# Exp in a windowed attention: the order in which its input is read and its output is written

## The chip, the cores and the metric

The kernel runs on one core of one Trainium2 chip. The metric is the device time of one launch in microseconds (us). "Before" was timed in six runs. One further execution was recorded by the hardware profiler; every duration, wait and timeline row below comes from that one.

## The reference, cut to what matters

Eight batches of eight heads, 576 positions, 64 values per head. Each position attends to the positions at most 32 away. The attention output, 4608 tokens of 512 values, goes through a two-layer network.

```python
scores = (1/sqrt(64)) * q @ k.T
scores = where(abs(pos_q - pos_k) <= 32, scores, -1e9)
attn   = exp(scores - max(scores));  attn = attn / (sum(attn) + 1e-9)
x      = attn @ v                    # -> 4608 tokens x 512
h      = x @ w_in                    # 512 -> 2048
g      = s * relu(h)**2 + b
out    = g @ w_out                   # 2048 -> 512
```

The kernel leaves out the subtraction of the maximum (the scores are small) and divides by the sum after the product with v.

## The kernel before, in words

**Attention.** A unit (`unit(b, m)`, L534) makes up to 128 tokens of batch `b`; a batch has five units, and eight batches make 40. A unit has an even key tile and, except in the last unit of a batch, an odd one, of 64 keys each. For a key tile, TensorE (PE) multiplies the keys of a pair of heads, laid out block-diagonally in `KBD` so that 2 x 64 keys fill the 128 partitions, with the queries of its window `QT`: four matmuls (L543), one for each pair of heads, into one of the two banks of the PSUM tile `SC`. A window has 128 queries, or 96 in the first and last tile of a batch. ScalarE (ACT) then takes the exponential of the whole bank and writes bf16 into the SBUF tile `EXE` (even) or `EXO` (odd): this is L560, the line that changes, 72 instructions in all. In batches 2 to 7 VectorE (DVE) multiplies the result by the band mask in place (L564); in batches 0 and 1 the mask was added beforehand by a matmul (L549). PE multiplies the weights with v into `AVN` (L582; 8 or 12 matmuls to a unit); DVE takes the reciprocal of the sums (L592) and scales (L595); the result is transposed into `XT`, the input of the network: by PE and an ACT copy (L604, L607) for batches 0 and 1, by a DMA (L612) later.

**Why the queries are in two runs.** The queries are loaded two to a partition, and the two are transposed apart. `QT` therefore holds the even queries of a batch first and the odd ones after them (index `i`), and the matmul leaves a window's scores in PSUM in that order, for each pair of heads: `w/2` scores of the even queries, then `w/2` of the odd ones. The tiles `EXE` and `EXO`, the mask and everything after them have the queries in their natural order. L560 is the instruction that passes from the one order to the other.

**Network.** `s1` (L687): PE multiplies 512 tokens with 128 columns of `w_in` (4 matmuls, L698) into one of two PSUM banks `W`, ACT takes the relu into `R1` (L705), DVE squares it into `GT` (L707). `W` has two banks, so a group of L698 can start only when the relu of the group before last is done. `s2` (L711): PE multiplies `GT` with `w_out` in groups of 4 matmuls (L717) into `O`, DVE scales and adds a constant (L730), a DMA stores. The first three token blocks (128, 128 and 256 tokens) are worked while the weights still arrive; the other eight blocks have 512 tokens.

**Order.** Each of the five instruction streams has a fixed order, which is written at build time by a planner (`_Graph`) from costs given with each operation: for L560 the cost is `190 + 0.833 * 4 * w` (ns), where four pairs of `w` scores make one partition's elements. At run time every engine works through its stream in order and waits on semaphores. On the ACT stream exps stand between the relus and, in batches 0 and 1, between copies and casts (`qt` L479, `kbd` L490, `vbd` L445, `win` L419, `xt` L607).

Of the kernel before, what the change touches and what calls it, by code (L numbers as in the profile page):

```python
# [7 lines left out]
AF = mybir.ActivationFunctionType  # L8
# [34 lines left out]
class _Graph:  # L43
# [12 lines left out]
    def add(self, stream, fns, cost, reads=(), writes=(), key=0.0, accum=False, dma=None, waits=(),  # L56
            lat=None, slack=0.0):
        if not isinstance(fns, list):
            fns = [fns]
        t = _Task(len(self.tasks), stream, fns, cost, self.LAT[stream] if lat is None else lat, key,  # L60
                  dma, slack)
        t.deps.update(waits)
        for r in reads:
            assert r in self.writer, r
            t.deps.add(self.writer[r])
        for w in writes:
            if w in self.writer:
                t.deps.add(self.writer[w])
            if not accum:
                t.deps.update(self.readers.get(w, ()))  # L70
        t.deps.discard(t)
        for r in reads:
            self.readers.setdefault(r, []).append(t)
        for w in writes:
            self.writer[w] = t
            if not accum:
                self.readers[w] = []
        self.tasks.append(t)
        return t
# [157 lines left out]
def bass_sliding_window_symmetric__then__act_starrelu_kernel(  # L237
# [22 lines left out]
    with ExitStack() as es:  # L260
# [65 lines left out]
        def unit_rows(m):  # L326
            lo = max(0, 128 * m - WIN)
            return lo, min(S, 128 * m + 128 - WIN)

        def due(b, m):  # L330
            tok = b * S + unit_rows(m)[0]
            blk = next(x for x in range(NM) if TBLK[x][0] + TBLK[x][1] > tok)
            f = (tok - TBLK[blk][0]) / TBLK[blk][1]
            before = PH[blk] - PH[blk - 1] if blk > 0 else 4.0
            return PH[blk] - 14.0 - (1.0 - f) * before
# [62 lines left out]
        def pieces(lo, hi, step):  # L398
            return range(lo // step, (hi - 1) // step + 1)
# [131 lines left out]
        def xt_res(t0, t1):  # L531
            return [("XT", x % (XR // 32)) for x in range(t0 // 32, t1 // 32)]

        def unit(b, m):  # L534
            slot, key = b % 2, due(b, m)
            n = ucount["n"]
            ucount["n"] += 1
            ei, pi = n % NEX, (n - 1) % NEX
            tiles = [j for j in (2 * m, 2 * m + 1) if j < NTILE]
            for j in tiles:  # L540
                lo, hi = max(0, 64 * j - WIN), min(S, 64 * j + 64 + WIN)
                c0, w, par = lo - (64 * j - WIN), hi - lo, j % 2
                fns = [lambda e, j=j, pr=pr, lo=lo, hi=hi, w=w, par=par: e.matmul(  # L543
                    SC[:, par, pr * 128:pr * 128 + w],
                    lhsT=KBD[:, pr, j, :], rhs=QT[slot][:, :, pr, lo // 2:hi // 2], start=b > 1,
                    stop=b > 1 or pr == NPAIR - 1) for pr in range(NPAIR)]
                src = SC[:, par, :].rearrange("p (a c) -> p a c", c=128)[:, :, 0:w]
                if b < 2:
                    fns.insert(0, lambda e, src=src, c0=c0, w=w: e.matmul(  # L549
                        src.rearrange("p a (i c) -> p a i c", i=2), lhsT=IDENT[:, :],  # L550
                        rhs=MASKB.rearrange("p a (i c) -> p a i c", i=2)[:, :, :, c0 // 2:(c0 + w) // 2],
                        start=True, stop=False))
                add("pe", fns, (8 if b < 2 else 4) * (w / 2.4 + 3.0),
                    reads=[("QT", slot, x, i) for x in pieces(lo, hi, 64) for i in (0, 1)]
                    + [("KBD", j, p0, i) for p0 in (0, 64) for i in (0, 1)]
                    + (["IDENT"] + [("MASKB", pr) for pr in range(NPAIR)] if b < 2 else []),
                    writes=[("SC", par)], key=key, slack=1500.0)
                src = src.rearrange("p a (i c) -> p a i c", i=2)
                dst = (EXE[ei][:, :, c0:c0 + w], EXO[ei][:, :, 64 + c0:64 + c0 + w])[par]
                add("act", lambda e, src=src, dst=dst: e.activation(  # L560
                    dst.rearrange("p a (c i) -> p a i c", i=2), src, AF.Exp, bias=0.0, scale=0.125),
                    190 + 0.833 * 4 * w, reads=[("SC", par)], writes=[("E", ei, par)], key=key)
                if b > 1:
                    add("dve", lambda e, dst=dst, c0=c0, w=w: e.tensor_tensor(  # L564
                        dst, dst, MASK[:, :, c0:c0 + w], ALU.mult),
                        130 + 0.53 * 4 * w, reads=[("E", ei, par), "MASK"], writes=[("E", ei, par)], key=key)
            r0, r1 = unit_rows(m)
            nr = r1 - r0
            lead = 0 if r0 == 128 * m - WIN else WIN
            av, avr = AVN, ["AVN"]  # L570
            if b == 0 and m % 2:
                av, avr = O.rearrange("p i (a c) -> p (i a) c", a=2), [("O", 0), ("O", 1)]
            fns = []
            for pr in range(NPAIR):
                parts = []
                if m > 0:
                    parts.append((EXO[pi], 128, 2 * m - 1))
                parts.append((EXE[ei], lead, 2 * m))
                if 2 * m + 1 < NTILE:
                    parts.append((EXO[ei], lead, 2 * m + 1))  # L580
                for x, (buf, col, j) in enumerate(parts):
                    fns.append(lambda e, pr=pr, buf=buf, col=col, j=j, x=x, last=len(parts) - 1: e.matmul(  # L582
                        av[0:nr, pr, 0:130], lhsT=buf[:, pr, col:col + nr],
                        rhs=VBD[slot][:, j, pr, 0:130], start=(x == 0), stop=(x == last)))
            vx = {int(j > 3) for j in tiles} | ({int(2 * m - 1 > 3)} if m > 0 else set())
            add("pe", fns, len(fns) * 57.0,
                reads=[("E", ei, j % 2) for j in tiles] + ([("E", pi, 1), ("EXZ", pi, 192)] if m > 0 else [])
                + [("EXZ", ei, 0), ("EXZ", ei, 192)] + [("V", slot, p0, x) for p0 in (0, 64) for x in vx]
                + [(r, slot, p0) for r in ("VBDZ", "VBDO") for p0 in (0, 64)], writes=avr, key=key)
            land["av", b, m] = g.tasks[-1]  # L590
            ri, xi = n % 2, n % NXN
            add("dve", lambda e: e.reciprocal(REC[ri][0:nr, :].rearrange("p (a b) -> p a b", b=2),  # L592
                                              av[0:nr, :, 128:130]),
                210, reads=avr, writes=[("REC", ri)], key=key)
            add("dve", lambda e: e.tensor_tensor(  # L595
                XN[xi][0:nr, :].rearrange("p (a b c) -> p a b c", a=4, b=2),
                av[0:nr, :, 0:128].rearrange("p a (b c) -> p a b c", b=2),
                REC[ri][0:nr, :].rearrange("p (a b one) -> p a b one", b=2, one=1).to_broadcast((nr, 4, 2, 64)),
                ALU.mult),
                680, reads=avr + [("REC", ri)], writes=[("XN", xi)], key=key)  # L600
            x0 = b * S + r0
            if b < 2:
                view = av.bitcast(BF16)[:, :, 384:512]
                add("pe", [lambda e, pr=pr: e.transpose(  # L604
                    view[:, pr, 0:nr], XN[xi][0:nr, pr * 128:(pr + 1) * 128], IDENT[0:nr, 0:nr])
                    for pr in range(NPAIR)], 300, reads=[("XN", xi), "IDENT"], writes=avr, key=key)
                add("act", lambda e: e.copy(XT[:, :, x0:x0 + nr], view[:, :, 0:nr]), 190 + 0.833 * 4 * nr,  # L607
                    reads=avr, writes=xt_res(x0, x0 + nr), key=key)
            else:
                cuts = [x0] + [x for x in range(XR, B * S, XR) if x0 < x < x0 + nr] + [x0 + nr]  # L610
                for a0, a1 in zip(cuts, cuts[1:]):
                    add("sp", lambda e, a0=a0, a1=a1: e.dma_start(  # L612
                        XT[:, :, a0 % XR:a0 % XR + a1 - a0], XN[xi][a0 - x0:a1 - x0, :], transpose=True),
                        1250.0, reads=[("XN", xi)], writes=xt_res(a0, a1), key=key,
                        dma=("t", (a1 - a0) // 4, 22.0))
# [3 lines left out]
        def attention():  # L619
# [26 lines left out]
            for m in range(NUNIT):  # L646
                unit(0, m)
# [194 lines left out]
```

The softmax here doesn't subtract the row's maximum and nothing guards it: scores larger than these inputs give would overflow.

## Time and profile before

| | |
|---|---|
| median of six runs | 334.57 us (332.94 to 335.73) |
| the profiled execution: time | 332.46 us |
| the profiled execution: span from first to last instruction | 330.7 us |
| granted TensorE clock | 1.00 |
| PE busy | 308.4 us, 93% of the span |
| DVE busy | 207.5 us, 63% |
| ACT busy | 166.3 us, 50% |
| GpSimd (POOL) busy | 87.9 us, 27% |

The span and 1.8 us around it make the time of the profiled execution, which is 2.1 us under the median of the six. A busy share is an average over the whole span; three stretches differ. Up to 78 us the weights and the first two batches are loaded and PE has gaps; from 78 to 270 us attention and network run together; after 270 us only the network is left. In the rows below, a group of instructions shows "out<-in", the shapes as partitions x elements, the count, then busy us and mean ns of one, and last the idle time ahead of it with what ended it. In a timeline row the first number is the start, the second the length of the merged instructions, both in us.

### The profile page before, as it was taken

To read this page: it belongs to the slowest core of one execution; us is meant where nothing else is said; L and a number is where in the kernel's file an instruction comes from. 1 tells how busy PE (TensorE), PEld (TensorE's weight loads), DVE (VectorE), ACT (ScalarE), POOL (GpSimd) and SP (SyncE) were. 2 spreads that over 40 slices of the span, in tenths; PEclk is the share of its full clock that TensorE was granted. 3 is DMA by queue.
4 is the path that set the end of the run, shared out by engine and by line. 5 is a ranking of instruction groups with operands and counts; after the bars stand their busy time and mean duration, and the time that the engine had idled before them with its cause. 6 is when DMAs were issued, how large, how long until landed. Compare 5 with 4: busy or idle time off the path is not lost.

```text
span 330.7 us, 5874 instructions
## 1 busy us (share of the span) xinstructions
PE 308.4 (93%) x2234; PEld 178.2 (54%) x2234; DVE 207.5 (63%) x485; ACT 166.3 (50%) x270; POOL 87.9 (27%) x136
## 2 busy tenths in 40 slices
PE   1678899698999999999999999999999999999995
PEld 1467797585554556455545555555555554444442
DVE  6555775268877786888688768765874453333411
ACT  6696388328562655557175655444644433333300
POOL 8562343750920236034305500450000000000000
PEclk9999999999999999999999999999999999999999
DMA  8999999897999699969999996989911111000021
GB/s 211 224 358 356 250 236 287 216 242 170 213 196 211 171 232 204 242 140 224 214 228 164 227 213 144 254 162 214 147 53 58 55 44 64 33 32 34 32 94 66
DMA packets 107836, 57.15 MB, mean 173 GB/s; under 512 B 56608, under 2 KB 100128, under 8 KB 107808
## 3 DMA queue, kind: packets, MB, share of 16 engines
q1 hardware_dynamic: 103200, 49.69, 67.3%
q0 software_dynamic: 4608, 7.08, 11.1%
q8 instruction: 17, 0.28, 0.3%
q14 instruction: 11, 0.09, 0.1%
HBM read 36.70 MB, written 9.44 MB: 140 GB/s over the span
## 4 chain that ended last, share of the span: by engine, by line
PE 72%; DMA 10%; POOL 7%; SPq 4%; ACT 3%; DVE 2%; issue 1%; POOLq 0%; ACTq 0%
PE o L717 31%; PE w L698 31%; DMA stg<-in_moe_w_out_dram 6%; PE avn L582 5%; DMA vst<-in_v_dram 4%; POOL vst L432 4%; PE sc L543 3%; SPq L432 2%; POOL vbd L339 1%; ACT vbd L445 1%; DVE gt L707 1%; SPq L456 1%; ACT kbd L490 1%; SPq L416 0%; ACT qt L479 0%
## 5 line engine op out<-in xcount | busy, mean ns | idle before, releaser
L717 PE MATMUL o<-wout,gt 128*128 128x512 bf16 (+1 forms) x640 | 141.9, 358 | 3.6 <-DVE outs L730 2.7
L698 PE MATMUL w<-xt,win 128*128 128x512 bf16 (+2 forms) x704 | 143.1, 340 | 0.8 <-ACT r L705 0.8
L705 ACT ACTIVATE r<-w 128x512 bf16<-128x512 f32 x144 | 85.3, 598 | 95.1 <-PE w L698 80.6
L707 DVE TENSOR_TENSOR gt<-r 128x512 bf16<-128x512 bf16 x144 | 62.0, 438 | 54.0 <-ACT r L705 53.2
L717 PEld LDWEIGHTS o<-wout,gt 128*128 128x128 bf16 x640 | 61.1, 98 | 62.1 <-DVE outs L730 3.4
L698 PEld LDWEIGHTS w<-xt,win 128*128 128x128 bf16 x704 | 61.6, 98 | 51.9 <-ACT r L705 1.6
L432 POOL DMA_DIRECT2D vst<-in_v_dram x96 | 59.7, 630 | 104.0 <-PE avn L582 55.4
L730 DVE SCALAR_TENSOR_TENSOR outs<-o,sb,cvec 128x512 f32<-128x512 f32 (+1 forms) x40 | 27.7, 693 | 21.5 <-PE o L717 17.6
L560 ACT ACTIVATE exe<-sc 128x512 bf16<-128x512 f32 (+1 forms) x40 | 27.5, 689 | 17.1 <-PE sc L543 16.5
L582 PE MATMUL avn<-vbd,exo 128*128 128x130 bf16 (+1 forms) x240 | 27.6, 220 | 2.2 <-ACT xt L607 2.2
L595 DVE TENSOR_TENSOR xn<-avn,rec 128x512 bf16<-128x512 f32 (+1 forms) x38 | 26.1, 687 | 2.2 <-DMA xt<-xn 1.3
L582 PE MATMUL avn<-vbd,exe 128*128 128x130 bf16 (+1 forms) x152 | 25.1, 219 | 0.5 <-ACT vbd L445 0.5
L543 PEld LDWEIGHTS sc<-qt,kbd 128*128 128x128 bf16 x288 | 20.2, 99 | 9.7 <-issue 0.7
L560 ACT ACTIVATE exo<-sc 128x512 bf16<-128x512 f32 x32 | 23.8, 742 | 3.1 <-PE sc L543 3.0
L445 ACT CAST vbd<-vst 64x1024 bf16<-64x1024 f32 (+1 forms) x15 | 16.5, 1140 | 17.2 <-DMA vst<-in_v_dram 17.1
L582 PEld LDWEIGHTS avn<-vbd,exo 128*128 128x128 bf16 (+1 forms) x240 | 21.8, 104 | 6.0 <-ACT xt L607 2.5
L543 PE MATMUL sc<-qt,kbd 128*128 128x128 bf16 (+1 forms) x288 | 24.5, 218 | 0.0
L506 DVE CAST nat<-stg 128x1024 bf16<-128x1024 f32 (+1 forms) x36 | 23.7, 680 | 0.0
L521 DVE COPY kbd<-kt 64x512 bf16<-64x512 bf16 (+1 forms) x72 | 19.1, 266 | 0.8
L582 PEld LDWEIGHTS avn<-vbd,exe 128*128 128x128 bf16 (+1 forms) x152 | 16.0, 108 | 3.8 <-ACT vbd L445 0.8
L564 DVE TENSOR_TENSOR exe<-exe,mask 128x512 bf16<-128x512 bf16 (+1 forms) x30 | 11.7, 391 | 7.1 <-ACT exe L560 7.0
L592 DVE RECIPROCAL rec<-avn 128x8 f32<-128x8 f32 (+1 forms) x38 | 7.7, 204 | 12.4 <-PE avn L582 12.0
(63 smaller groups left out, 136.6 us busy)
## 6 DMA issues: line engine op xcount, KB each, us to landing
stg<-in_q_dram SPq DMA_DIRECT2D x16, 512.0 KB, 5.3
stg<-in_k_dram SPq DMA_DIRECT2D x16, 512.0 KB, 7.4
out_dram<-outs SPq DMA_DIRECT2D x32, 256.0 KB, 2.5
vst<-in_v_dram POOLq DMA_DIRECT2D x96, 72.0 KB, 5.4
stg<-in_moe_w_in_dram SPq DMA_DIRECT2D x8, 512.0 KB, 8.8
stg<-in_moe_w_out_dram SPq DMA_DIRECT2D x8, 512.0 KB, 9.3
vst<-in_v_dram SPq DMA_DIRECT2D x16, 144.0 KB, 4.7
stg<-in_q_dram SPq DMA_DIRECT2D x8, 128.0 KB, 6.3
```

The costliest lines, as they stand in the source:

```text
L432: add(stream, lambda e, dst=dst, src=src: e.dma_start(dst, src), 640.0 if stream == "sp" else 700.0, writes=[("VST", h, x) for x in (range ...
L445: add(eng, (lambda e, dst=dst, src=src: e.copy(dst, src)) if eng == "act" else (lambda e, dst=dst, src=src: e.tensor_copy(dst, src)), {"ac ...
L506: add("dve", lambda e, si=si, ni=ni: e.tensor_copy(NAT[ni][0:n, :, :].rearrange("p i (h d) -> p h i d", h=H), STG[si][0:n, 0:1024].rearran ...
L543: fns = [lambda e, j=j, pr=pr, lo=lo, hi=hi, w=w, par=par: e.matmul(SC[:, par, pr * 128:pr * 128 + w], lhsT=KBD[:, pr, j, :], rhs=QT[slot] ...
L560: add("act", lambda e, src=src, dst=dst: e.activation(dst.rearrange("p a (c i) -> p a i c", i=2), src, AF.Exp, bias=0.0, scale=0.125), 190 ...
L582: fns.append(lambda e, pr=pr, buf=buf, col=col, j=j, x=x, last=len(parts) - 1: e.matmul(av[0:nr, pr, 0:130], lhsT=buf[:, pr, col:col + nr] ...
L595: add("dve", lambda e: e.tensor_tensor(XN[xi][0:nr, :].rearrange("p (a b c) -> p a b c", a=4, b=2), av[0:nr, :, 0:128].rearrange("p a (b c ...
L698: add("pe", [lambda e, g=g, kc=kc: e.matmul(wt[:, g, :], lhsT=WIN_BF[:, kc, (f0 + g) * 128:(f0 + g + 1) * 128], rhs=XT[:, kc, t0 % XR:t0 % ...
L705: add("act", lambda e: e.activation(rt, wt, AF.Relu, bias=0.0, scale=1.0), 190 + 0.833 * 512, reads=[("W", wb)], writes=[("R1", rb)], key=key)
L707: add("dve", lambda e: e.tensor_tensor(GT[gs][:, f0:f0 + ng, g0:g0 + nt], rt, rt, ALU.mult), 130 + 0.53 * 512, reads=[("R1", rb)], writes= ...
L717: add("pe", [lambda e, fc=fc: e.matmul(O[:, ob, 0:cn], lhsT=GT[gs][:, fc, g0:g0 + 128], rhs=WOUT_BF[:, fc, c0:c0 + cn], start=(fc == 0), s ...
L730: add("dve", lambda e: e.scalar_tensor_tensor(OUTS[us][:, 0:cn], O[:, ob, 0:cn], SB128[:, 0:1], CVEC[:, c0:c0 + cn], ALU.mult, ALU.add), 2 ...
```

## The change

The loop over a bank's scores is turned. Before, the exp goes through PSUM in the order in which the scores lie there (pair of heads, even or odd, query) and writes each run at a step of two elements, since the even and the odd queries interleave in the output. After, it goes through the output in its own order (pair of heads, query), which is contiguous in SBUF, and reads the scores alternately from the even and the odd run: consecutive elements are `w/2` fp32 values apart in PSUM, which is 256 bytes for a window of 128 queries and 192 bytes for one of 96. The number of instructions, the elements of each, their tiles, types and function, and the cost that the planner is given are the same.

```diff
-                src = src.rearrange("p a (i c) -> p a i c", i=2)
+                src = src.rearrange("p a (i c) -> p a c i", i=2)
                 dst = (EXE[ei][:, :, c0:c0 + w], EXO[ei][:, :, 64 + c0:64 + c0 + w])[par]
                 add("act", lambda e, src=src, dst=dst: e.activation(
-                    dst.rearrange("p a (c i) -> p a i c", i=2), src, AF.Exp, bias=0.0, scale=0.125),
+                    dst.rearrange("p a (c i) -> p a c i", i=2), src, AF.Exp, bias=0.0, scale=0.125),
                     190 + 0.833 * 4 * w, reads=[("SC", par)], writes=[("E", ei, par)], key=key)
```

## The prediction

> **What bounds the kernel now.** I read the busy shares first, then the stages, because one share over the whole span hides where a wait counts.
>
> ```profile
> PE 308.4 (93%) x2234; PEld 178.2 (54%) x2234; DVE 207.5 (63%) x485; ACT 166.3 (50%) x270; POOL 87.9 (27%) x136
> ...
> PE 72%; DMA 10%; POOL 7%; SPq 4%; ACT 3%; DVE 2%; issue 1%; POOLq 0%; ACTq 0%
> ```
>
> ```profile
> 0.00:78.00 78.00, 59.36 (x691) 49.73 (x691) 47.04 (x101) 49.11 (x79) 38.50 (x56) 1.00 1.05 265
> 78.00:270.00 192.00, 191.94 (x1281) 102.76 (x1282) 141.86 (x349) 102.28 (x167) 49.35 (x80) 1.00 0.89 174
> ```
>
> The second fence is the view of busy time by stretch: stretch, length, then PE, weight loads, DVE, ACT and POOL, the granted clock, the DMA share. From 78 to 270 us PE is busy 191.94 of 192 us: nothing that another engine does faster can shorten this stretch by more than the missing 0.06 us and the small gaps that the pipelined records hide, but every wait that another engine puts on PE lengthens it one for one, since PE's order is fixed. ACT, which carries the changed line, is busy 102 of these 192 us. Up to 78 us the DMA share is 1.05: transfers set the pace there. Of the whole chain that ended last, ACT holds 3%.
>
> Next, the groups of ACT by shape:
>
> ```profile
> L705 ACT ACTIVATE r<-w 128x512 bf16<-128x512 f32 x144 | 85.3, 598 | 95.1 <-PE w L698 80.6 <-DVE outs L730 11.3 <-DVE gt L707 2.4
> L560 ACT ACTIVATE exo<-sc 128x512 bf16<-128x512 f32 x32 | 23.8, 742 | 3.1 <-PE sc L543 3.0
> L560 ACT ACTIVATE exe<-sc 128x512 bf16<-128x512 f32 x24 | 17.9, 746 | 7.2 <-PE sc L543 6.7
> L560 ACT ACTIVATE exe<-sc 128x384 bf16<-128x384 f32 x16 | 9.7, 603 | 9.9 <-PE sc L543 9.7
> ...
> L490 ACT COPY kbd<-o 64x512 bf16<-64x512 bf16 x4 | 2.6, 718 | 1.0 <-PE o L473 1.0
> L607 ACT COPY xt<-avn 128x512 bf16<-128x512 bf16 x4 | 2.3, 584 | 6.4 <-PE avn L604 6.4
> ```
>
> The relu (L705) has the same 512 elements, source and types as the exp, contiguous on both sides, and takes 598 ns; the exp, writing at a step of two, takes 742. The other line that writes at a step of two is the copy L490: 718 ns against 584 for a contiguous copy of 512. So the step of two costs about 140 ns of 512 elements, whatever the function.
>
> The length of a row is not what it holds the engine for, since ACT instructions overlap. The starts tell that, in the two places where exps stand closest to a PE wait:
>
> ```profile
> 79.57 0.60 ACT L560 ACTIVATE exe<-sc 128x384 bf16<-128x384 f32 x1
> 80.03 0.72 ACT L560 ACTIVATE exo<-sc 128x512 bf16<-128x512 f32 x1
> 80.61 0.58 ACT L705 ACTIVATE r<-w 128x512 bf16<-128x512 f32 x1
> ...
> 81.25 1.04 PE L698 MATMUL w<-xt,win 128*128 128x512 bf16 x4
> ```
>
> ```profile
> 111.13 0.60 ACT L705 ACTIVATE r<-w 128x512 bf16<-128x512 f32 x1 [0.27 <-PE w L698]
> ...
> 111.62 0.74 ACT L560 ACTIVATE exe<-sc 128x512 bf16<-128x512 f32 x1
> 112.21 0.74 ACT L560 ACTIVATE exo<-sc 128x512 bf16<-128x512 f32 x1
> ...
> 112.78 1.11 ACT L705 ACTIVATE r<-w 128x512 bf16<-128x512 f32 x2
> ...
> 113.55 0.81 PE L698 MATMUL w<-xt,win 128*128 128x512 bf16 x3
> ```
>
> Start to start, an exp of 512 holds ACT for 0.59 us (111.62 to 112.21), one of 384 for 0.46, a relu for 0.49 (111.13 to 111.62).
>
> **The change: what goes.** The stepped write goes: 0.59 becomes 0.49 us, if the read costs nothing; 0.10 x 56 + 0.07 x 16, some 7 us of ACT time. Almost none of it lies on the path: PE alone covers it after 78 us.
>
> **What comes.** The read now jumps 256 (or 192) bytes from element to element. No ACT row of the trace reads PSUM in jumps, so the cost is bounded from both sides. From below: nothing, 0.49 us. The nearest row is the stepped write itself: if the jumping read costs what that did, the exp stays at 0.59 and nothing changes. A rule of the Trainium skill speaks against the change. In "SBUF — State Buffer", section "Specifications (TRN2)", full rate needs two hits on one line; lines are 16 bytes in SBUF, which hold eight bf16 elements, and 8 bytes in PSUM, two fp32 values. By this rule the old write, four elements to a line, was free, and the new read, one to a line, is not. The trace contradicts the first half (742 against 598 ns), so I take the rule as too mild; its second half nothing here shows. If full rate takes two hits, one hit gives half the rate, an estimate: 0.83 ns more for each element (the relu's 0.83 comes from the xt copies, 584 and 480 ns for 512 and 384), 0.43 us for 512. "Vector Engine (DVE) Microarchitecture Reference", section "5.2 Measured stream behaviour on trn2 (trn3 not measured)", gives numbers for VectorE in SBUF: 1.05 ns an element contiguous, 1.73 when one source hops at every element, 2.50 when it steps by 24 words, but full rate for a stream that alternates between two regions. As estimates for 512 elements: +0.35, +0.74 or 0 us. I take half the rate, which lies between the first two: an exp of 512 holds ACT for 0.49 + 0.43 = 0.92 us and takes 598 + 427 = 1025 ns; one of 384 holds it for 0.71. Against before that is d = +0.33 us (+0.25 for 384) in the engine, +0.28 in length. By the trace's nearest row alone the sum would be 0, by the rule it is what follows.
>
> **Where it lands.** Everything else keeps its place: on PE, DVE, POOL and the DMA queues the order is the same, and ACT has the same rows in the same order. Behind an exp wait the next relu on ACT (and behind that PE's next L698 group in that W bank), the mask on DVE and then PE's L582.
>
> Up to 78 us: five exps between 15.94 and 20.69 us stand in a full ACT stream, ahead of the casts of v (18.16) and w_in (21.18), and push them by up to 5 x 0.33 = 1.6 us. The w_in cast frees a staging buffer at 22.22, but the w_out load that takes it is issued only at 25.43, after an issue that holds SP's queue for 4.36 us: 3.2 us of cover. PE stands idle 1.5 us at 29.0, 0.9 at 35.6 (for a w_out load) and 2.7 at 60.8. The units of batch 1 have 6 us or more between their last exp and L582. The v load that lands at 75.1 starts the long stretch; no exp is ahead of it. Cost 0; were the cover gone, 1.6 us.
>
> From 78 us, by spare times read from the timeline:
> - 81.25 us: the relu at 80.61 stands behind two exps; its PE group was done at 80.29. The next group in that bank starts 0.04 us after the relu's end, which is the mere handoff: spare 0. Cost 0.25 + 0.33 = 0.58.
> - 113.55: the relu at 112.78 ends 113.38, spare 0.13 beyond the handoff. The pair before it (109.18, 109.64) delays the relu at 110.26 and leaves ACT 0.16 late at 111.62; two exps add 0.66. Cost 0.16 + 0.66 - 0.13 = 0.69.
> - L582: from the mask's end to the first matmul, the spare of the tightest units is 0.40 (batch 2, unit 0; covered by the first item's shift), 0.52 (batch 5, unit 2), 0.60 (batches 2 and 4, unit 2), 0.62 and 0.68; the others have more. A pair of exps takes 0.33 + 0.28 = 0.61: cost 0.09 + 0.01 + 0.01.
> - The other relus behind exps have 0.5 to 2.4 us: 0.02.
>
> Sum +1.4 us. After 270 us there is no exp. On the profiled execution: 332.46 + 1.4 = 333.9; it is 2.1 us under the median of the six, so for the median 334.57 + 1.4 = 336.0 us.
>
> **The rivals.** (1) The read is free, or as dear as the old write. For it: the alternating stream at full rate. Then ACT gains at most 0.10 us an exp, and PE gains the gap ahead of 81.25 us (0.1 us) and nothing else: 334.5 us. Were the 5 x 0.10 us before 20.7 us to reach the w_out load, 334.0; the SP issue speaks against it. A gain of over 0.5% (1.7 us; also about what a measurement of this kernel can tell from no change) has no place in this profile.
> (2) The jump is much dearer, and ACT becomes PE's releaser throughout. At 2.4 times the contiguous time (the 24-word step) an exp of 512 holds ACT 1.23 us, d = 0.64, a pair 1.24 us late. That is over the spare of nearly every unit: 1.1 at 81.25, 1.9 around 111 to 114, and at ten further places 0.2 to 0.7, 5 together: +8 us, 342.6 us. It decides from d = 0.37, where a pair passes the 0.6 to 0.8 us of spare that most units have; below, only the two relus count.
> (3) The change does not do what it says, because the access is turned back when it is built: the built instruction does write contiguous rows of 128 (or 96) and 512, so I give this, 334.6 us, no chance of its own.
>
> **How the numbers follow.** Half rate, +0.8 to +2.2 us: 0.42. Free or like the write: 0.25. Dearer: 0.33. Half rate lies astride the bound of 1.7 us: I put 0.26 of it within and 0.16 above. Faster 0.02 and same 0.23 out of the second case. Together faster 0.02, same 0.49, slower 0.49. The range runs from 333.9 (rival 1, with some scatter) to 343.0 (rival 2); the likeliest case alone 335.4 to 336.8.
>
> **What would show it.** L560 near 1025 ns for 512 elements and 0.92 us start to start; new rows "PE w L698 <- ACT r L705" near 81 and 113 us; little change elsewhere. L560 near 600 ns: rival 1. Near 1340 ns, and PE L582 waiting for DVE's masks in most batches: rival 2. Wrong altogether if the time moves while L560 does not, or if the first 78 us grow.

## The result, and the profile after

The changed kernel took 333.69 us in the median of 28 runs, the kernel before 334.19 us in 63 runs: ratio 0.9984, 95% interval 0.9966 to 1.0003. Two further comparisons, made with experiments below, gave 0.9974 (0.9943 to 1.0006) and 0.9978 (0.9949 to 1.0006). No one of them is clear of 1; all three lie on the same side, near 0.2% or 0.7 us. The ratios leave out executions more than 1.5% above the fastest of their kernel and are not the quotients of the medians. It is no change, with at most a very small gain, and not the 336.0 us that was predicted: the measured time lies 0.2 us under the range.

The profiled execution of the changed kernel took 333.87 us, its span is 332.1 us. The busy shares and the chain by engine, from its page:

```profile
PE 310.4 (93%) x2234; PEld 179.5 (54%) x2234; DVE 206.7 (62%) x485; ACT 159.8 (48%) x270; POOL 87.4 (26%) x136
...
PE 79%; DMA 10%; SPq 4%; ACT 3%; POOL 2%; DVE 1%; issue 1%; ACTq 0%
```

ACT fell from 166.3 to 159.8 us. PE, which sets the end, is busy 310.4 us instead of 308.4; the 2 us lie ahead of 76.8 us, where its clock was lower (below). The groups of ACT by shape show where the 6.5 us went:

```profile
L705 ACT ACTIVATE r<-w 128x512 bf16<-128x512 f32 x144 | 85.8, 599 | 99.5 <-PE w L698 86.1 <-DVE outs L730 11.3 <-DVE gt L707 1.1
L560 ACT ACTIVATE exo<-sc 128x512 bf16<-128x512 f32 x32 | 19.2, 601 | 4.8 <-PE sc L543 4.7
L560 ACT ACTIVATE exe<-sc 128x512 bf16<-128x512 f32 x24 | 14.4, 598 | 9.0 <-PE sc L543 8.8
...
L560 ACT ACTIVATE exe<-sc 128x384 bf16<-128x384 f32 x16 | 7.9, 491 | 10.5 <-PE sc L543 10.5
```

The exp now takes what the relu takes: 598 to 601 ns for 512 elements where it took 742 to 746, 491 for 384 where it took 603. These rows show no cost of the read in jumps. Where the prediction looked first, the timeline of ACT and PE now reads:

```profile
80.69 0.49 ACT L560 ACTIVATE exe<-sc 128x384 bf16<-128x384 f32 x1
81.06 0.61 ACT L560 ACTIVATE exo<-sc 128x512 bf16<-128x512 f32 x1
81.53 0.62 ACT L705 ACTIVATE r<-w 128x512 bf16<-128x512 f32 x1
...
82.33 1.03 PE L698 MATMUL w<-xt,win 128*128 128x512 bf16 x4
```

The relu starts 0.84 us after the first exp instead of 1.04. It ends, 0.62 us after its start, 0.18 us ahead of the L698 group that takes its bank; before, that group started 0.05 us after the relu's end (the prediction has 0.04). This wait is gone, but it was worth little: from the start of the L698 group ahead of it (79.26 before, 80.38 after) the group now comes after 1.95 us instead of 1.99.

The long stretch, from the first L698 group of 512 tokens to the last L582, is 193.3 us in the profile before (75.09 to 268.36) and 193.0 us after (76.77 to 269.76). The difference cannot be put down to the exps. At the start of the stretch L698 waits for a relu, 0.84 us before and 0.28 us after; after, it waits another 0.44 us at 140.92, which it does not before. In all three places the relu stands behind casts of v (L445).

The start of the stretch, 75.1 and 76.8 us, goes with the granted TensorE clock ahead of it. This is the clock's row of the two pages, before and then after, with one digit for a fortieth of the span:

```profile
PEclk9999999999999999999999999999999999999999
PEclk9999999799999999999999999999999999999999
```

From 60 to 70 us the clock is 1.00 before and 0.83 after. Up to the start of the stretch PE is busy 57.3 us before and 59.4 us after, with 678 matmuls in both.

### The profile page after: what moved, and what is told of

It reads as the page before. It is cut to its first block, busy times and chain, and to the rows that moved or that the text cites. A ratio compares the mean times of both kernels' runs of the same rounds, so it can differ in the third digit from the quotient of the medians.

```text
span 332.1 us, 5874 instructions
## 1 busy us (share of the span) xinstructions
PE 310.4 (93%) x2234; PEld 179.5 (54%) x2234; DVE 206.7 (62%) x485; ACT 159.8 (48%) x270; POOL 87.4 (26%) x136
## 4 chain that ended last, share of the span: by engine, by line
PE 79%; DMA 10%; SPq 4%; ACT 3%; POOL 2%; DVE 1%; issue 1%; ACTq 0%
PE o L717 34%; PE w L698 33%; PE avn L582 6%; DMA stg<-in_moe_w_out_dram 4%; PE sc L543 4%; DMA out_dram<-outs 2%; SPq L432 2%; DMA vst<-in_v_dram 2%; DMA stg<-in_moe_w_in_dram 2%; SPq L456 2%; PE o L740 1%; POOL vst L432 1%; ACT vbd L445 1%; ACT r L705 1%; DVE outs L730 0%
## 5 line engine op out<-in xcount | busy, mean ns | idle before, releaser
L698 PE MATMUL w<-xt,win 128*128 128x512 bf16 (+2 forms) x704 | 143.2, 340 | 0.7 <-ACT r L705 0.7
L707 DVE TENSOR_TENSOR gt<-r 128x512 bf16<-128x512 bf16 x144 | 61.0, 431 | 55.1 <-ACT r L705 54.4
L698 PEld LDWEIGHTS w<-xt,win 128*128 128x128 bf16 x704 | 61.7, 98 | 51.9 <-ACT r L705 1.5
L560 ACT ACTIVATE exe<-sc 128x512 bf16<-128x512 f32 (+1 forms) x40 | 22.2, 555 | 19.5 <-PE sc L543 19.4
L582 PE MATMUL avn<-vbd,exo 128*128 128x130 bf16 (+1 forms) x240 | 27.6, 220 | 2.2 <-ACT xt L607 2.2
L595 DVE TENSOR_TENSOR xn<-avn,rec 128x512 bf16<-128x512 f32 (+1 forms) x38 | 26.1, 687 | 3.0 <-DMA xt<-xn 2.1
L582 PE MATMUL avn<-vbd,exe 128*128 128x130 bf16 (+1 forms) x152 | 25.1, 219 | 0.5 <-ACT vbd L445 0.5
L543 PE MATMUL sc<-qt,kbd 128*128 128x128 bf16 (+1 forms) x288 | 25.2, 222 | 0.0
L582 PEld LDWEIGHTS avn<-vbd,exo 128*128 128x128 bf16 (+1 forms) x240 | 21.8, 104 | 5.8 <-ACT xt L607 2.5
L445 ACT CAST vbd<-vst 64x1024 bf16<-64x1024 f32 (+1 forms) x15 | 16.5, 1139 | 16.0 <-DMA vst<-in_v_dram 15.9
L560 ACT ACTIVATE exo<-sc 128x512 bf16<-128x512 f32 x32 | 19.2, 601 | 4.8 <-PE sc L543 4.7
L582 PEld LDWEIGHTS avn<-vbd,exe 128*128 128x128 bf16 (+1 forms) x152 | 16.0, 108 | 3.6 <-ACT vbd L445 0.6
```

Source lines behind the costliest of these rows:

```text
L445: add(eng, (lambda e, dst=dst, src=src: e.copy(dst, src)) if eng == "act" else (lambda e, dst=dst, src=src: e.tensor_copy(dst, src)), {"ac ...
L560: add("act", lambda e, src=src, dst=dst: e.activation(dst.rearrange("p a (c i) -> p a c i", i=2), src, AF.Exp, bias=0.0, scale=0.125), 190 ...
L595: add("dve", lambda e: e.tensor_tensor(XN[xi][0:nr, :].rearrange("p (a b c) -> p a b c", a=4, b=2), av[0:nr, :, 0:128].rearrange("p a (b c ...
L698: add("pe", [lambda e, g=g, kc=kc: e.matmul(wt[:, g, :], lhsT=WIN_BF[:, kc, (f0 + g) * 128:(f0 + g + 1) * 128], rhs=XT[:, kc, t0 % XR:t0 % ...
L707: add("dve", lambda e: e.tensor_tensor(GT[gs][:, f0:f0 + ng, g0:g0 + nt], rt, rt, ALU.mult), 130 + 0.53 * 512, reads=[("R1", rb)], writes= ...
```

## The experiments

Two questions: what a jump costs, in the read and in the write, and what a slower exp would have cost.

**e1: no reordering at all.** Here and in e2, e3, e9 and e10 only L558 and L561 differ from the changed kernel.

```diff
-                src = src.rearrange("p a (i c) -> p a c i", i=2)
-                    dst.rearrange("p a (c i) -> p a c i", i=2), src, AF.Exp, ...
+                    dst, src, AF.Exp, ...
```

> Read and write both contiguous: the exponents stay in the order in which the scores lie (even queries, then odd ones), so the mask and the product with v meet them in the wrong order; every instruction and its size is kept. Theory F (ScalarE reads PSUM in jumps at its full rate, and only the stepped write of the kernel before cost anything): L560 takes what it takes in the changed kernel, 598 to 601 ns for 512 elements and 491 for 384, within 5 ns. Theory P (the jump costs something, but less than the step in the write did): 10 to 30 ns less than in the changed kernel. The time is that of the changed kernel in both, near 334 us.

Its groups by shape:

```profile
L560 ACT ACTIVATE exo<-sc 128x512 bf16<-128x512 f32 x32 | 19.3, 602 | 4.6 <-PE sc L543 4.5
L560 ACT ACTIVATE exe<-sc 128x512 bf16<-128x512 f32 x24 | 14.3, 597 | 8.7 <-PE sc L543 8.5
```

602 and 597 ns, against 601 and 598 with the jumping read. Theory F holds; theory P, that some smaller cost is left, falls. One run took 333.56 us.

**e2: one stream at a step of 32 bytes.**

```diff
-                src = src.rearrange("p a (i c) -> p a c i", i=2)
-                    dst.rearrange("p a (c i) -> p a c i", i=2), src, AF.Exp, ...
+                src = src.rearrange("p a (c i) -> p a i c", i=8)
+                    dst.rearrange("p a (i c) -> p a i c", i=8), src, AF.Exp, ...
```

> The exp reads PSUM at a step of eight fp32 values (32 bytes), one plain strided stream instead of two that alternate, and writes contiguous runs; the exponents come out permuted, counts and sizes are kept. Theory F: 598 to 601 ns for 512 elements again, 491 for 384. Theory A (the changed kernel's read is free because only two runs alternate, each of which goes on where it stopped; a stream that leaves its line at every element is not): at half the rate 1025 ns for 512, at 1.3 times the contiguous time of an element about 740. Under A at half the rate the time rises by about 1.4 us, under F it stays near 334 us.

```profile
L560 ACT ACTIVATE exo<-sc 128x512 bf16<-128x512 f32 x32 | 19.2, 599 | 3.6 <-PE sc L543 3.5
L560 ACT ACTIVATE exe<-sc 128x512 bf16<-128x512 f32 x24 | 14.3, 595 | 7.2 <-PE sc L543 7.0
```

Again the contiguous time; one run took 331.69 us. So it is not the alternation between two runs that makes the read free (theory A): neither an alternating read 256 bytes apart nor a plain step of 32 bytes is slower than a contiguous one.

**e3: the mirror image, a write in jumps.**

```diff
-                src = src.rearrange("p a (i c) -> p a c i", i=2)
-                    dst.rearrange("p a (c i) -> p a c i", i=2), src, AF.Exp, ...
+                src = src.rearrange("p a (c i) -> p a c i", i=2)
+                    dst.rearrange("p a (i c) -> p a c i", i=2), src, AF.Exp, ...
```

> The mirror image: the exp reads PSUM contiguously and writes bf16 alternately into two runs, w/2 elements (128 or 96 bytes) apart; the exponents come out permuted, counts and sizes are kept. Theory W (ScalarE's write wants neighbours: a write that does not fill up the word of the element before it costs 0.28 ns an element, whatever the distance): 740 to 750 ns for 512 elements, as with the step of two. Theory W2 (the cost of a write grows with the distance, since every element goes to another line): more, up to half the rate, 1025 ns. Theory W3 (only the step within one line is slow, alternating runs are free as they are in the read): 600 ns.

The run took 414.89 us. Its groups, and from its waits after 78 us the two largest of TensorE (one wait, seen at the weight loads and at the matmuls):

```profile
L560 ACT ACTIVATE exo<-sc 128x512 bf16<-128x512 f32 x32 | 87.1, 2722 | 1.2 <-PE sc L543 1.2
L560 ACT ACTIVATE exe<-sc 128x512 bf16<-128x512 f32 x24 | 59.9, 2496 | 4.2 <-PE sc L543 4.1
L560 ACT ACTIVATE exe<-sc 128x384 bf16<-128x384 f32 x16 | 31.3, 1957 | 11.4 <-PE sc L543 11.4
...
L564 DVE TENSOR_TENSOR exo<-exo,mask 128x512 bf16<-128x512 bf16 x24 | 10.2, 426 | 39.4 <-ACT exo L560 39.4
```

```profile
PEld avn L582 <- DVE exo L564: 29.2, 17, 3.2
PE avn L582 <- DVE exo L564: 21.8, 13, 2.8
```

No theory was near: 2500 to 2720 ns are some 4 ns an element over the contiguous write, where even W2 allowed 0.83. With such an exp ACT does become TensorE's releaser: PE waits for the mask, and the mask for the exp. That is the mechanism of rival 2 of the prediction, reached by the write instead of the read.

**e9 and e10: which part of such a write is dear.**

```diff
# e9: pairs of elements, jumps of 256 (EXE) or 512 bytes (EXO)
+                src = src.rearrange("p a (c x) -> p c a x", x=2)
+                    dst.rearrange("p a (c x) -> p c a x", x=2), src, AF.Exp, ...
# e10: a plain step of 16 bytes
+                src = src.rearrange("p a (i c) -> p a i c", i=8)
+                    dst.rearrange("p a (c i) -> p a i c", i=8), src, AF.Exp, ...
```

> The kernel with the write in jumps of 128 bytes took 2500 to 2720 ns for an exp of 512. Here the exp writes two neighbouring bf16 elements, one whole aligned 4-byte word, and then jumps 256 or 512 bytes to the next pair of heads, reading PSUM in the same order; the exponents stay in run order, counts and sizes are kept. Theory H (it is the half-filled word that is dear: an element that does not complete its word waits for it, and the two halves of a word come apart in time): whole words cost little, 600 to 750 ns for 512. Theory D (it is the distance from one write to the next): 1300 to 2700 ns, half to all of the cost of single elements in jumps. Under H the time is that of the changed kernel, under D it is 345 us or more.

> The exp reads PSUM contiguously and writes bf16 at a step of eight elements, 16 bytes, in plain strided streams of 16 (or 12); the exponents come out permuted, counts and sizes are kept. Theory H (the half-filled word is dear only when its other half is written soon after, as in the alternating write, where it comes two elements later): like the step of two, about 740 ns for 512, since the other half of a word comes 16 elements later. Theory D (the distance is dear): far more, 1000 to 2700 ns. Theory L (cost by how many elements share 16 bytes: four at a step of two, one here): between, 1000 to 1300 ns.

First e9, then e10:

```profile
L560 ACT ACTIVATE exo<-sc 128x512 bf16<-128x512 f32 x32 | 19.9, 621 | 4.6 <-PE sc L543 4.5
L560 ACT ACTIVATE exe<-sc 128x512 bf16<-128x512 f32 x24 | 14.9, 620 | 8.5 <-PE sc L543 8.4
```

```profile
L560 ACT ACTIVATE exo<-sc 128x512 bf16<-128x512 f32 x32 | 86.7, 2709 | 1.3 <-PE sc L543 1.3
L560 ACT ACTIVATE exe<-sc 128x512 bf16<-128x512 f32 x24 | 59.6, 2482 | 4.2 <-PE sc L543 4.2
```

Whole words in jumps cost 20 ns in 512 elements (334.6 us), so distance alone is not dear: theory D falls. Single bf16 elements at a step of 16 bytes cost what they cost in jumps of 128 (412.64 us), so theory H's 740 ns for e10 falls as well, and with it the thought that the other half of the word must follow soon; L's 1000 to 1300 ns are too low too. Dear is a single element whose neighbour in the stream lies far: 4 bytes away (the kernel before) it costs 0.28 ns, 16 and 128 bytes away about 4. Whether the filled word decides is not shown: the two elements of a pair in e9 share a word, but they are also two in a row within the same 16 bytes, as the four of the kernel before are, while in e3 and e10 each element goes to other 16 bytes than the one ahead of it. A step of 8 bytes, with two half-filled words in 16 bytes, would part the two; nothing between 4 and 16 bytes was tried, and why it is so these runs do not show.

**e4: other reads in jumps.**

```diff
-                    dst = VBD[...].rearrange("p t a c -> p (t a) c")
-                    src = VST[...].rearrange("p t a c -> p (t a) c")
+                    dst = VBD[...].rearrange("p t a c -> p (t a) c").rearrange("p n (c i) -> p n c i", i=2)
+                    src = VST[...].rearrange("p t a c -> p (t a) c").rearrange("p n (i c) -> p n c i", i=2)
...
-            add("dve", lambda e: e.scalar_tensor_tensor(OUTS[us][:, 0:cn], O[:, ob, 0:cn], SB128[:, 0:1],
+                OUTS[us][:, 0:cn].rearrange("p (c i) -> p c i", i=2),
+                O[:, ob, 0:cn].rearrange("p (i c) -> p c i", i=2), SB128[:, 0:1],
```

> Where did the figures hold on which the prediction's half rate rested? The exp is as in the changed kernel. Two other reads are turned to jumps, both with contiguous writes: the cast of v (L445 on ScalarE, L446 on VectorE and GpSimd) reads fp32 from SBUF alternately from two runs of 32 in each 64, and the scaling of the output (L730 on VectorE) reads fp32 from PSUM alternately from two runs of 256. The columns of v and of the output come out permuted; counts and sizes are kept. In the changed kernel: L445 1042 ns for 1024 elements and 1251 for 1280; L730 693 ns in the mean over its two sizes. Theory F (the distance of a read costs nothing on ScalarE, in SBUF as in PSUM): L445 unchanged within 10 ns. Theory S (it is PSUM that is free, SBUF is not): L445 up by 0.25 to 0.83 ns an element, 1300 to 1900 ns for 1024. For VectorE, theory F: L730 unchanged; theory V (VectorE pays 0.68 ns an element): L730 up by about 300 ns in the mean, and VectorE's casts up by 0.7 to 1.3 us.

```profile
L445 ACT CAST vbd<-vst 64x1280 bf16<-64x1280 f32 x7 | 10.8, 1537 | 0.0
L445 ACT CAST vbd<-vst 64x1024 bf16<-64x1024 f32 x8 | 10.1, 1267 | 18.1 <-DMA vst<-in_v_dram 18.1
...
L730 DVE SCALAR_TENSOR_TENSOR outs<-o,sb,cvec 128x512 f32<-128x512 f32 x32 | 23.9, 746 | 16.1 <-PE o L717 15.9
L446 DVE CAST vbd<-vst 64x1280 bf16<-64x1280 f32 x8 | 6.5, 816 | 0.0
L446 DVE CAST vbd<-vst 64x1024 bf16<-64x1024 f32 x8 | 5.5, 690 | 6.2 <-DMA vst<-in_v_dram 6.2
```

In the changed kernel the same rows have 1251, 1042, 746, 805 and 680 ns. ScalarE pays 0.22 ns an element (225 over 1024) for a jumping read of SBUF, though it pays none in PSUM: a little under theory S. VectorE reads PSUM in jumps for nothing, and its casts from SBUF lose 10 ns: theory F, and V falls. GpSimd has one such cast, of 1280 elements, which took 2095 ns instead of 1819. The one run took 334.69 us, but the 3.8 us more of L445 on ACT were not all hidden: the long stretch is 196.4 us in its profile, the longest with exps of this length, and L698 waits 1.5 us at 141.0 for a relu behind casts of v.

**e5 and e6: what a slower exp costs.** Every exp runs twice, first into a scratch tile, in the changed kernel (e5) and in the kernel before (e6).

```diff
+        SCR = [sb((128, 4, 128), BF16, "scr") for _ in range(4)]
...
+                k = 2 * (n % 2) + par; twice = [SCR[k][:, :, 0:w]]
-                add("act", lambda e, src=src, dst=dst: e.activation(
-                    dst.rearrange("p a (c i) -> p a c i", i=2), src, AF.Exp, bias=0.0, scale=0.125),
+                add("act", [lambda e, src=src, to=to: e.activation(
+                    to.rearrange("p a (c i) -> p a c i", i=2), src, AF.Exp, bias=0.0, scale=0.125) for to in twice + [dst]],
```

> The changed kernel, with every exp run twice: first into a scratch tile, then into its own; all else and the order as before. An exp of 512 then holds ScalarE for 2 x 0.49 = 0.98 us instead of the 0.59 of the kernel before. This tests the second half of the prediction's sum, what a slower exp costs, apart from its wrong first half. By the prediction's spare times: 0.70 us at the relu near 81 us, 0.90 around 109 to 114, 0.9 at units whose spare a pair (0.74 us late) passes: +2.3 us on the kernel before, ratio 1.007. Rival: the spares add up to nothing, since delays swallow one another or a late unit is taken up by the next gap: within 0.2% of the kernel before. Second rival: the first 78 us are not covered: +4 us or more, 1.012.

> The kernel before, with every exp run twice, both with the stepped write: 2 x 0.59 = 1.18 us for 512 elements, d = 0.59 us an exp, and a pair is 1.18 us late. By the prediction's spare times nearly every unit now stops TensorE: 1.05 us near 81 us, 1.55 around 109 to 114, 0.2 to 0.7 at thirteen further places, 7.7 us in all, ratio 1.023 (327 to 342 us). Rival: the sum of spare times is too high, as one delay moves what comes after it: half of that, 1.012. Second rival: ScalarE at 60% of the span has room, and the time stays within 0.3%.

Measured: e5 336.26 us, ratio 1.001 (0.9967 to 1.0053); e6 340.9 us, in only four runs, ratio 1.0174 (1.012 to 1.0229). The profiled executions of both had a lower TensorE clock ahead of 78 us (0.93 in that stretch), so only the long stretch is read, where it was 1.00: it takes 195.6 us in e5 and 201.7 in e6, against 193.3 before. That is +2.4 and +8.4 us, where the sums of spare times gave +2.3 and +7.7. In e5 so close an agreement is in part luck: eight profiles in which an exp of 512 takes about 600 ns and runs once after 78 us (after, e1, e2, e7, e8, e9, e11, e12) lie between 192.5 and 194.7 us, so that e5 is only 0.9 us above the highest of them. e6 is 7 us above it. TensorE's largest waits for weight loads from 78 us on, before, then in e5, then in e6:

```profile
PEld w L698 <- ACT r L705: 1.6, 3, 1.0
PEld avn L582 <- DVE exe L564: 0.6, 1, 0.6
```

```profile
PEld avn L582 <- DVE exo L564: 2.6, 7, 0.6
PEld w L698 <- ACT r L705: 2.3, 5, 0.8
```

```profile
PEld avn L582 <- DVE exo L564: 6.0, 10, 1.0
PEld w L698 <- ACT r L705: 4.1, 6, 1.1
```

The largest two in e5 and e6 are those that the prediction named, the mask ahead of L582 and the relu ahead of L698. L698 stops at the two places that it named: PE's matmuls wait 0.58 us at each in e5 and 0.92 and 1.00 us in e6, where 0.70 and 0.90, then 1.05 and 1.55 were expected. The places at L582 fit less well. Unit 2 of batch 5 stops in e5 as listed, but units 2 of batches 2 and 4, listed among the tightest, stop only in e6. The wait for `exe` before (0.6 us, unit 4 of batch 6) is missing from the prediction's list: there the mask stands behind copies on DVE, not behind its exp. And 2.2 us of weight-load waits in e6 are for L595, the scaling that frees `AVN`, which the prediction leaves out.

In the whole time less is seen: e6 costs 1.2 to 2.3%, which takes in 7.7 us of 334 (2.3%) only at its edge, and e5's 0.7% lies outside its interval. The profile of the kernel before is a quick execution, 332.46 us against a median of 334.98 in the runs beside e5 and e6, so profile and time do not compare the same thing. "ScalarE has room, nothing happens" is refuted by e6; that the whole of the stretch's loss reaches the end is not shown.

**e7 and e11: only the exps ahead of 78 us twice, and e8 and e12: the changed kernel again.**

```diff
-                k = 2 * (n % 2) + par; twice = [SCR[k][:, :, 0:w]]
+                k = 2 * (n % 2) + par; twice = [SCR[k][:, :, 0:w]] if b < 2 else []
```

> The changed kernel, with only the 18 exps of batches 0 and 1 (all before 78 us) run twice, +0.49 us each. The prediction gave these exps no cost at all, as transfers set the pace up to 78 us and TensorE stands idle there. Theory C (covered): within 0.2% of the changed kernel, 333.7 us, and L698 of the first 512-token block still begins at 75 to 77 us in the profile. Rival: the five exps in the full ScalarE stream between 16 and 21 us push the loads of w_out, and 5 x 0.49 = 2.4 us come through: ratio 1.006 to the kernel before.

> The changed kernel once more, beside the same runs of the kernel before, to place the three kernels above against both and for a second profile of it. Ratio 0.998, between 0.996 and 1.001; L560 at 598 to 601 ns for 512 elements; and the start of the first 512-token block of the network (75.1 us in the profile of before, 76.8 in that of after) wherever the loads put it, 74 to 78 us, with no tie to the exps.

> The kernel with the 18 exps of batches 0 and 1 run twice came out at a ratio of 0.995 to the kernel before, 0.997 for the changed kernel beside it. Theory C (these exps are covered, the rest is scatter of the loading stage): 0.9975 within 0.002, not to be told from the changed kernel run beside it. Theory G (a later start of the network gives the loads room and gains time): 0.993 to 0.996, clearly under the changed kernel.

> The changed kernel beside the one above. Ratio 0.998 to the kernel before, 0.996 to 1.000. The change takes 0.10 us of each exp of 512 off ScalarE; by the prediction's places only the gap ahead of the relu near 81 us gives it back, 0.1 us or 0.03%, and up to 0.5 us (0.15%) if the earlier exps help the loads.

Measured: e7 0.9946 (0.9921 to 0.9971) beside e8 0.9974 (0.9943 to 1.0006); e11 0.997 (0.9947 to 0.9993) beside e12 0.9978 (0.9949 to 1.0006). The 18 exps in the loading stage cost nothing that can be told, though in the profile of e7 the first L582 starts at 20.29 us and the first L698 at 26.02, instead of 19.06 and 23.85 in the profile after: the cover holds, theory C. Their executions also show a lower granted clock, 0.988 (e7) and 0.989 (e11) in the mean against 0.993 (e8) and 0.994 (e12), without a longer time; why is not shown. The intervals of each pair overlap, so that theory G, a gain from the delay, is not shown.

The start of the long stretch was 74.6 us in e8, 77.5 in e12, 76.3 in e7, 78.6 in e11. It goes with the clock from 60 to 70 us and not with the exps: in the twelve profiles other than those of e3 and e10 it lies at 74.2 to 75.4 us where this clock was 1.00 (before, e2, e4, e6, e8), at 76.1 to 77.5 where it was 0.83 (after, e1, e7, e9, e12) and at 78.0 to 78.6 where it was 0.66 (e5, e11). That is 4 us of scatter in which 0.7 us are sought. What lowers the clock there was not tested.

## Why the prediction was right or wrong

- **What bounds the kernel: right.** PE is busy 192.3 of the 193.0 us of the long stretch, before 192.4 of 193.3; 6.5 us of ACT time went, and the one gap where 0.1 us was to be had gave 0.04.
- **What goes: right.** An exp of 512 holds ACT for 0.48 us now (112.69 to 113.17 in the timeline after, below), 0.49 was given; one of 384 for 0.37 (80.69 to 81.06), 0.39 was given.

```profile
112.69 0.59 ACT L560 ACTIVATE exe<-sc 128x512 bf16<-128x512 f32 x1
113.17 0.61 ACT L560 ACTIVATE exo<-sc 128x512 bf16<-128x512 f32 x1
```

- **What comes: wrong, and this is the step that failed.** "I take half the rate" put 0.43 us on the read of an exp of 512. It is 0: 601 and 598 ns in jumps, 602 and 597 contiguous (e1), 599 and 595 at a step of 32 bytes (e2). The Trainium skill's rule on lines ("SBUF — State Buffer", section "Specifications (TRN2)") was taken for ScalarE's reads of PSUM, and it does not hold for them in any order tried. The alternating stream at full rate, which the prediction quoted and set aside, was nearer to this access, though for another engine and memory. (The 2.50 ns quoted beside it, on which rival 2 was sized, is in the table of "Vector Engine (DVE) Microarchitecture Reference", section "5.2 Measured stream behaviour on trn2 (trn3 not measured)", for both sources or the output stepping by 24 words, not for one source.) The bound from below, "nothing", was the true value; the choice of the value between the bounds was the error. With it the predicted 336.0 us become 334.5, rival 1, which had a chance of 0.25.
- **The old write: right on the trace, and more than right.** The prediction held the trace against the rule that a step of two is free. The half rate that it took from the rule for a read of one element to a line, 1025 ns, is far too little for a write: e10's write at a step of 16 bytes takes 2482 to 2709 ns, over four times the contiguous row. This was not foreseen.
- **Where it lands: right in the kind of wait, in part in the places.** TensorE stops at the two relus, and at masks, though not at all the units listed, with 2.4 and 8.4 us in the long stretch against 2.3 and 7.7 from the sums; only e6's is clear of scatter. In the whole time e6 shows some 6 us and e5 nothing that can be told, which stays open.
- **The first 78 us: right.** Exps 0.49 us longer there (e7, e11) are not seen, and exps 0.10 us shorter gave nothing that can be told. In the profile after, the first L698 started 0.35 us earlier, but SP's queue was not: the row of its three w_out issues, before and then after, ends at 29.41 and 29.77 us.

```profile
21.03 8.38 SPq L416 DMA_DIRECT2D stg<-in_moe_w_out_dram  x3
```

```profile
20.71 9.06 SPq L416 DMA_DIRECT2D stg<-in_moe_w_out_dram  x3
```

- **The range** ended at 333.9 us, which is rival 1 less some scatter; the measured 333.69 us lies under it. The kernel before itself came out 0.4 us lower in the larger set of runs (334.19 instead of 334.57), so the lower end had too little room even for the case that it named.

Open: whether the change gains 0.2% at all. Three comparisons point that way, none is clear of 1. e7 and e11, which have the changed read too, are clear of it, but not of the changed kernel beside them. The long stretch, 193.0 us in the first profile after, 194.7 in e8 and 193.7 in e12 against 193.3 before, gives no place for 0.7 us.

## What to carry to other kernels

When ScalarE must reorder data on its way from PSUM to bf16 in SBUF, put the jumps on the read and keep the write contiguous, or at least write whole 4-byte words: here a reorder of 512 elements cost 0, 0.14 or 2 us an instruction by which side jumped and how. Before a rule on access patterns enters a sum, ask on which engine, which memory and which side it was measured, and let the bound that no trace row excludes keep its weight. And time freed on an engine at 50% was worth nothing here, where another is full, while time added to it (0.59 us an exp in e6, with the engine busy 59% of the span) was paid where it passed the spare time of single instructions, long before the engine was full.

## What the runs showed of the hardware that was not expected

- ScalarE reads fp32 from PSUM at full rate in every order tried: contiguous, two alternating runs 256 bytes apart, a step of 32 bytes (595 to 602 ns for 512 elements). VectorE too, for two alternating runs 1 KB apart (746 ns in both).
- From SBUF, ScalarE loses 0.22 ns an element when it alternates between two runs 128 bytes apart (1042 to 1267 ns for 1024 fp32), VectorE's cast 10 ns in all.
- ScalarE's bf16 write into SBUF, 512 elements: contiguous 598 ns; pairs in jumps 620; single elements 4 bytes apart 742; 16 bytes apart 2482 to 2709; alternating between runs 128 bytes apart 2496 to 2722. The last two brought the whole kernel to 412.64 and 414.89 us, in one run each.
- From 60 to 70 us the granted TensorE clock was 1.00, 0.83 or 0.66 in profiles of nearly the same work, and the stretch behind it started at 74.2 to 75.4, 76.1 to 77.5 or 78.0 to 78.6 us.
